# Moving work and stores between engines in a four-layer attention and GLU training kernel

What was changed: the first block of a GLU stage is turned on PE instead of by DMA; stores of turned tiles are issued by SyncE, one later; the transposed load of the down weights is cut in three; small attention weight gradients are made in the tail; copies of attention backward run on ScalarE.

## The chip, the cores and the metric

The kernel runs on one core of one Trainium2 chip. The metric is the device time of one execution in microseconds (us), as the median of several runs. The profile is of one execution. In it PE is TensorE (matmuls), PEld its weight loads, DVE VectorE, ACT ScalarE, POOL GpSimd, SP SyncE. SyncE and POOL also issue DMA transfers. A tile whose name ends in `_ps` lies in PSUM, the memory that this kernel's matmuls write and sum in; "turned" means transposed; the granted clock is the share of full speed at which PE was allowed to run.

## The reference

Four residual layers, forward and backward: linear attention, GLU, linear attention, GLU, with the same weights in both attentions and in both GLUs. The outputs are the result and the gradients of x and of the five weights. Everything is bfloat16. S = 2048, D = 512, F = 1376, 32 heads of 16.

```python
phi = lambda t: jnp.where(t > 0, t + 1, jnp.exp(t)) + 1e-6
pq, pk = phi(q), phi(k)
kv  = jnp.einsum("bhsd,bhse->bhde", pk, v)
z   = jnp.einsum("bhsd->bhd", pk)
num = jnp.einsum("bhqd,bhde->bhqe", pq, kv)
den = jnp.einsum("bhqd,bhd->bhq", pq, z)[..., None] + 1e-6
attention = (num / den)...reshape(B, S, D) @ wo          # cut
glu = (sigmoid(x @ w_gate) * (x @ w_up)) @ w_down

x = A_x
x = x + attention(layernorm(x))      # layer 0
x = x + glu(layernorm(x))            # layer 1
x = x + attention(layernorm(x))      # layer 2
x = x + glu(layernorm(x))            # layer 3
# the kernel also returns the vjp of all this for grad_out
```

## The kernel before

The sequence is cut into 4 blocks of 4 tiles of 128 rows. Most products of the kernel take a normalised block turned (`hT`), and forward stores many tiles in DRAM for backward. Four parts matter here.

Layer norm after the first layer: POOL makes the negated mean and the power, ACT the squares, DVE applies, and a transposing DMA issued by SyncE turns the block. `pooled` ties stores issued by POOL (`k.st` is POOL) to POOL's powers and products.

```python
            neg = k.small.tile([P, 2], F32, name="ln_neg", bufs=8)
            nc.gpsimd.tensor_scalar(neg[:], k.sums[st // 2][:], -1.0 / D, None, ALU.mult)
            # cut: ScalarE squares and sums with bias=neg
            nc.gpsimd.tensor_scalar(rstd, ss[:], 1.0 / D, EPS_LN, ALU.mult, ALU.add)
            pooled(k, nc.gpsimd.tensor_tensor(rstd, rstd, k.neghalf[:], ALU.pow))
            for i in range(2):
                nc.vector.tensor_scalar(self.h[b][:, j - 1 + i, :], k.xs[st - 1 + i][:], neg[:, i:i + 1],
                                        rstd[:, i:i + 1], ALU.add, ALU.mult)
            nc.sync.dma_start_transpose(out=self.hT[b][:, j - 1:j + 1].rearrange("p a c q -> p (a c) q"),
                                        in_=self.h[b][:, j - 1:j + 1, :].rearrange("p a d -> p (a d)"))
```

Attention's query features and the normalised features `qn`, which a DMA turns and which POOL stores when they have landed:

```python
        nc.vector.tensor_scalar(a_t[:], pe[:, 1], 1.0, EPS, ALU.min, ALU.add)
        nc.gpsimd.tensor_scalar(pe[:, 1], pe[:, 1], 1.0, None, ALU.min)
        for i in range(2):
            nc.vector.scalar_tensor_tensor(pe[:, 0, i, :], qs[i][:], 1.0 + EPS, a_t[:, i, :], ALU.add, ALU.max)
        # cut, in share():
        nc.sync.dma_start_transpose(out=self.qn[b][:, 2 * d2:2 * d2 + 2].rearrange("p c a q -> p (c a) q"),
                                    in_=pe[:, 0].rearrange("p c s -> p (c s)"))
        if d2:
            self.turned.append((self.sv["qn"][b], self.qn[b]))
            self.store_turned()          # k.st.dma_start of the oldest waiting tile
```

GLU forward of layer 1 stores its slopes and products as soon as they are made:

```python
            hh, sd = glu(k, ln.hT[b], fc)
            nc.sync.dma_start(out=sv["sd"][b, fc], in_=flat(sd))
            store_hh(k, sv, b, fc, hh)   # k.st.dma_start, so POOL
```

Attention backward has a first pass over the blocks (gradients of the queries), a middle part (small matrices), and a second pass (gradients of the keys, values and the layer's input). The gradients of `wo` and of the value weights, which need only small products, are made at the start of the second pass. Layer 2 comes first and stores its share in `dwp`; layer 0 reads that share back and adds it:

```python
    for c in range(NDC):
        ps = k.ps.tile([P, D], F32, name="dw_ps", tag="bank")
        nc.tensor.matmul(ps[:], lhsT=kv[:, c, :], rhs=C[:, c, :], start=True, stop=True)
        put(k, ps[:], "wo", rows(c), slice(0, D), mode, stg)
    # cut: 4 transposes of dkv, then 16 matmuls and 4 more put for the value weights
def put(k, ps, nm, rs, cs, mode, pool=None):
    # cut
    if mode == "last":
        old = pool.tile([P, D], BF16, name="dw_old", **({} if pool is k.p_dst else dict(bufs=1)))
        nc.sync.dma_start(out=old[0:r, 0:w], in_=k.dwp[nm][rs, cs])
        nc.vector.tensor_tensor(new[0:r, 0:w], ps, old[0:r, 0:w], ALU.add)
    else:
        nc.scalar.copy(new[0:r, 0:w], ps)
    k.st.dma_start(out=dst, in_=new[0:r, 0:w])
```

After both backward attentions comes the tail, which is almost only matmuls of large weight gradients.

Of the kernel before, what the change touches and what calls it, by code (L numbers as in the profile page):

```python
# [16 lines left out]
D = 512  # L17
# [38 lines left out]
def kernel(  # L56
# [41 lines left out]
    for l in range(4):  # L98
        d = dict(h=dram.tile([S, D], BF16, name=f"sv_h{l}"))
        if l % 2 == 0:  # L100
# [6 lines left out]
            d["kv"] = dram.tile([P, NDC * P], BF16, name=f"sv_kv{l}")  # L107
        else:
# [8 lines left out]
    k.dwp = {nm: dram.tile(list(k.w_in[nm].shape), BF16, name=f"dwp_{nm}") for nm in k.w_in}  # L117
    k.rstd = [k.keep.tile([P, NST], F32, name=f"rstd{l}") for l in range(4)]
    k.A = {l: {} for l in (0, 2)}
    k.n_pool, k.waiting = 0, []  # L120
# [35 lines left out]
def build_mask(k):  # L156
    nc = k.nc

    after(k, nc.gpsimd.memset(k.bdmask[:], 1.0), k.last_pool)
# [35 lines left out]
def pooled(k, ins):  # L195

    k.n_pool += 1
    k.last_pool = ins
    while k.waiting and k.waiting[0][0] <= k.n_pool:
        after(k, k.st.dma_start(**k.waiting.pop(0)[1]), ins)  # L200


def store_later(k, lag=4, **kw):
    k.waiting.append((k.n_pool + lag, kw))
# [5 lines left out]
class LN:  # L210
# [12 lines left out]
    def one(self, st):  # L223
# [5 lines left out]
        if l == 0:  # L229
# [9 lines left out]
            if 0 < st < 6:  # L239
                after(k, add, k.last_pool)  # L240
            pooled(k, nc.gpsimd.tensor_tensor(rstd, rstd, k.neghalf[:, 0:1], ALU.pow))
# [9 lines left out]
        elif j % 2:  # L251
# [3 lines left out]
            nc.gpsimd.tensor_scalar(neg[:], k.sums[st // 2][:], -1.0 / D, None, ALU.mult)  # L255
# [6 lines left out]
            pooled(k, nc.gpsimd.tensor_tensor(rstd, rstd, k.neghalf[:], ALU.pow))  # L262
            for i in range(2):
                nc.vector.tensor_scalar(self.h[b][:, j - 1 + i, :], k.xs[st - 1 + i][:], neg[:, i:i + 1],
                                        rstd[:, i:i + 1], ALU.add, ALU.mult)
            nc.sync.dma_start_transpose(out=self.hT[b][:, j - 1:j + 1].rearrange("p a c q -> p (a c) q"),
                                        in_=self.h[b][:, j - 1:j + 1, :].rearrange("p a d -> p (a d)"))
        if j == NB - 1:
            k.st.dma_start(out=by_tile(k.sv[l]["h"], b * NB, NB), in_=self.h[b][:])
            if l % 2 == 0:  # L270
                store_later(k, out=k.sv[l]["hT"][b], in_=flat(self.hT[b]))
# [11 lines left out]
def forward(k):  # L283
    nc, tc = k.nc, k.tc
    with ExitStack() as ctx:
# [28 lines left out]
        for b, fc in b_both(k, 3, lns[3], ctx):  # L314
            if b == 0:
                next(second, None)
                if next(second, None) is None and actx:
                    actx.close()
                    wb = w_pool(k, "wb")
                    k.wuT = wb.tile([P, NFC, D], BF16, name="wuT")  # L320
                    k.wgT = wb.tile([P, NFC, D], BF16, name="wgT")
                    load_b_bwd(k, k.wuT, "wu", k.last_mul)
                    load_b_bwd(k, k.wgT, "wg", k.last_mul)
                    actx = None
        assert not k.waiting
# [18 lines left out]
def load_b_fwd(k, pks):  # L344
    nc, wd = k.nc, k.w_in["wd"]
    after(k, nc.gpsimd.memset(k.wd[0:FDUP, NFC - 1, :], 0.0), k.last_pool)
# [4 lines left out]
         nc.sync.dma_start(out=k.wd[FDUP:P, NFC - 1, :], in_=wd[n:F, :]))  # L351

# [16 lines left out]
class AFwd:  # L369


    def __init__(self, k, l, ln):
        self.k, self.l, self.ln, self.sv = k, l, ln, k.sv[l]
        self.pks, self.turned, self.pe, self.RD, self.qn, self.rd = [], [], {}, {}, {}, {}

    def store_turned(self):

        dst, t = self.turned.pop(0)
        self.k.st.dma_start(out=dst, in_=flat(t))

    def keys(self, st):
# [16 lines left out]
        if j == NB - 1:  # L398
            self.turned.append((self.sv["pkT"][b], self.pkT))
            if b:  # L400
                self.store_turned()
# [33 lines left out]
    def query(self, b, d2):  # L435
# [12 lines left out]
        nc.gpsimd.tensor_scalar(pe[:, 1], pe[:, 1], 1.0, None, ALU.min)  # L448
# [18 lines left out]
    def share(self, b, d2):  # L467
# [14 lines left out]
        if d2:  # L482
            self.turned.append((self.sv["qn"][b], self.qn[b]))
            self.store_turned()

    def slope(self, b, d2):
        k, pe = self.k, self.pe[b, d2]
        k.nc.vector.tensor_tensor(pe[:, 1], pe[:, 1], self.rd[b, d2][:], ALU.mult)
# [29 lines left out]
    def second(self, nxt):  # L518
# [36 lines left out]
        if l == 2:  # L555
            k.wdT = k.p_wa.tile([P, NDC, F], BF16, name="wdT", tag="wkvo")
            nc.sync.dma_start_transpose(out=k.wdT[:], in_=k.w_in["wd"])
# [15 lines left out]
        self.query(2, 1)  # L573
        self.out(1, 2, nxt)
        self.out(1, 3, nxt)
        self.slope(1, 1)
        self.den(2)
        yield True
# [8 lines left out]
        dst, t = self.turned.pop(0)  # L587
        store_later(k, out=dst, in_=flat(t))


def glu(k, hT, fc):
# [13 lines left out]
    pooled(k, nc.gpsimd.tensor_tensor(sd[:, 1, :], sd[:, 1, :], hh[:], ALU.mult))  # L605
# [3 lines left out]
def store_hh(k, sv, b, fc, hh):  # L609
    p0, f1 = (FDUP if fc == NFC - 1 else 0), min((fc + 1) * P, F)  # L610
    k.st.dma_start(out=sv["hhT"][fc * P:f1, b * SB:(b + 1) * SB], in_=hh[p0:P])


def b_fwd(k, l, ln, nxt):
    nc, sv = k.nc, k.sv[l]
    hhs = {}
# [9 lines left out]
    for b in range(NBLK):  # L626
        hhs[b] = []
        for fc in range(NFC):
            hh, sd = glu(k, ln.hT[b], fc)
            hhs[b].append(hh)  # L630
            nc.sync.dma_start(out=sv["sd"][b, fc], in_=flat(sd))
            store_hh(k, sv, b, fc, hh)
            if fc == 1 and b:
                down(b - 1)
            yield b, fc
    down(NBLK - 1)
# [10 lines left out]
def b_both(k, l, ln, ctx):  # L647
# [17 lines left out]
    for b in range(NBLK):  # L665
# [4 lines left out]
        for fc in range(NFC):  # L670
# [9 lines left out]
            store_hh(k, sv, b, fc, hh)  # L680
# [31 lines left out]
def backward(k):  # L712
    nc, tc = k.nc, k.tc
    with ExitStack() as ctx:
# [23 lines left out]
        k.p_set, k.p_dst = pool("dw_set_end", 6), pool("dw_stage_end", 6)  # L738
        for i, a in ((0, 1), (1, 0), (1, 1), (2, 0), (2, 1)):
            joint(i, a)  # L740
# [6 lines left out]
        for i, nm in ((1, "dkT"), (0, "dqT")):  # L747
            dw_cols(k, "wqkv", i * D, (0, D), [(h2, sv[2][nm]), (h0, sv[0][nm])])

# [77 lines left out]
def a_bwd(k, l, final):  # L827
    with ExitStack() as ctx:
        CT, dzp = a_bwd1(k, l, ctx)
        a_bwd2(k, l, final, ctx, CT, dzp)  # L830


def a_bwd1(k, l, ctx):
    nc, sv, A = k.nc, k.sv[l], k.A[l]
    big = ctx.enter_context(k.tc.tile_pool(name=f"ab_big{l}", bufs=1))
# [3 lines left out]
    k.big2 = ctx.enter_context(k.tc.tile_pool(name=f"ab_big2{l}", bufs=1))  # L839
    with k.tc.tile_pool(name=f"ab_ph1{l}", bufs=2) as ph1:  # L840
        CT_ps = [k.ps2.tile([P, D], F32, name="CT_ps", tag="dwbank") for _ in range(NDC)]
        late = []

        def sums(b, g_t, qn):
            for jc in range(NDC):
                for j in range(NB):
                    nc.tensor.matmul(CT_ps[jc][:], lhsT=g_t[:, j, jc * P:(jc + 1) * P], rhs=qn[:, :, j, :],
                                     start=(b == 0 and j == 0), stop=(b == NBLK - 1 and j == NB - 1))

        def soft(b, dc, dq, u_t, qp, rp, dqT):  # L850
            t_ps = k.ps.tile([P, SB], F32, name="t_ps", tag="bank")
            nc.tensor.matmul(t_ps[:], lhsT=k.bdmask[:], rhs=u_t[:], start=True, stop=True)
            w_t = ph1.tile([P, SB], BF16, name="w_t")
            nc.vector.scalar_tensor_tensor(w_t[:], t_ps[:], A["nz"][:, dc:dc + 1], dq[:], ALU.mult, ALU.add)  # L854
            nc.gpsimd.tensor_tensor(dqT[:, dc, :], w_t[:], rp[:, dc, :], ALU.mult)  # L855
            nc.vector.scalar_tensor_tensor(u_t[:], t_ps[:], -1.0, qp[:, dc, :], ALU.mult, ALU.mult,
                                           accum_out=dzp[:, dc, b:b + 1])
            if dc == NDC - 1:
                k.st.dma_start(out=by_chunk(sv["dqT"], b), in_=dqT[:])

        for b in range(NBLK):
            g_t = k.p_h.tile([P, NB, D], BF16, name="ga_t", tag="h_t")
            gT = k.p_hT.tile([P, NB, NDC, P], BF16, name="gaT_t", tag="hT_t")
            for j in range(NB):
                nc.scalar.copy(g_t[:, j, :], k.xs[b * NB + j][:])
                if j % 2 == 0:
                    tp = k.ps.tile([P, 2 * NDC, P], BF16, name="T_ps", tag="bank")
                for c in range(NDC):
                    nc.tensor.transpose(tp[:, j % 2 * NDC + c, :], g_t[:, j, c * P:(c + 1) * P], k.ident[:])
                if j % 2:  # L870
                    nc.scalar.copy(gT[:, j - 1:j + 1].rearrange("p a c q -> p (a c) q"), tp[:])
            qr = k.p_sh.tile([P, 2, NDC, SB], BF16, name="qr_l", tag="sh")
            qp, rp = qr[:, 0], qr[:, 1]
            nc.sync.dma_start(out=flat(qr), in_=sv["qr"][b])
            qn = k.p_h.tile([P, NDC, NB, P], BF16, name="qn_l", tag="h_t")
            nc.sync.dma_start(out=flat(qn), in_=sv["qn"][b])
            if b == 0 and l == 2:
                nc.sync.dma_start_transpose(out=k.woT[:], in_=k.w_in["wo"])
                nc.sync.dma_start_transpose(out=k.wqkvT[:], in_=k.w_in["wqkv"])
            if b == NBLK - 1 and l == 2:  # L880
                nc.sync.dma_start_transpose(out=k.wdT[:], in_=k.w_in["wd"])
            dqT = ph1.tile([P, NDC, SB], BF16, name="dqT_t")
            for dc in range(NDC):
                ps = k.ps.tile([P, SB], F32, name="dq_ps", tag="bank")
                mm4(k, ps[:], lambda c: MT[:, c, dc * P:(dc + 1) * P], lambda c: gT[:, :, c, :])
                dq = ph1.tile([P, SB], BF16, name="dq_sb", bufs=3)
                nc.scalar.copy(dq[:], ps[:])
                u_t = ph1.tile([P, SB], BF16, name="u_t", bufs=3)
                nc.vector.tensor_tensor(u_t[:], dq[:], qp[:, dc, :], ALU.mult)
                late.append((b, dc, dq, u_t, qp, rp, dqT))  # L890
                if len(late) > 2:
                    soft(*late.pop(0))
# [225 lines left out]
```

## Time and profile before

| | before |
|---|---|
| median of the first 3 runs | 1251.42 us (1248.57 to 1255.02) |
| profiled execution, span | 1240.5 us |
| PE busy, and not busy in the span | 1109.0 us, 131 us |
| mean granted PE clock | 0.968 |
| POOL busy | 454.0 us |

The page, its first part (busy us, share of the span) and two rows of its second part (the span in 40 slices, busy tenths, and the granted clock in tenths):

```profile
PE 1109.0 (89%) x5536; PEld 511.5 (41%) x5536; DVE 548.4 (44%) x968; ACT 513.2 (41%) x1020; POOL 454.0 (37%) x563
...
PE   5978899986697999999779799989799999999997
...
PEclk9998899999799999999999899999899899999999
```

PE is the limit almost everywhere; the dips (slices 10 and 11, and some single ones) are where time is to be had. The dips have a second price: after a wait of 6.8 us, which ended at 130.0 us, four matmuls took 1.86 us where four take 1.02 to 1.03 elsewhere, and the granted clock from 130 to 134 us was 0.50. The clock record of this trace holds only full and half, and 81 us of half (the mean of 0.968 alone would give 2 x 0.032 x 1240.5 = 79 us).

PE's waits (waiter, line and releaser: total us, times, longest us):

```profile
PE den_ps L458 <- DVE pe_t L450: 14.6, 5, 11.5
PE g_ps L179 <- DMA hT_t<-h_t: 11.5, 2, 8.3
PE u_ps L179 <- ACT rd_t L475: 7.4, 2, 6.8
...
PE dh_ps L704 <- DMA wgT<-in_B_w_gate_dram: 4.6, 1, 4.6
```

The list names only the last link of a chain. The timeline shows the chain (start us, duration us, engine and line, what, and in brackets the engine's idle time before it and what ended that). From layer 2 into layer 3, before:

```profile
306.23 0.64 POOL L379 DMA_DIRECT2D sv_qn_125<-qn_t  x1 [9.97 <-DMA qn_t<-pe_t]
...
308.72 1.28 DVE L264 TENSOR_SCALAR h_t<-x_90,ln_neg,rstd_140 128x512 bf16<-128x512 f32 x1 [7.68 <-POOL rstd_140 L262]
...
313.95 0.26 PE L458 MATMUL den_ps<-pe_t,Z_t 128*32 128x128 bf16 x1 [11.50 <-DVE pe_t L450]
...
314.66 2.03 SPq L266 DMA_TRANSPOSE hT_t<-h_t  x1
...
322.50 0.61 PE L179 MATMUL g_ps<-hT_t,wg 128*128 128x512 bf16 x1 [8.29 <-DMA hT_t<-h_t]
```

POOL stands for 10 us at a store whose tile is still being turned. The rest of the layer norm, with its power, stands right behind it in POOL's order, so DVE waits 7.7 us for it. DVE makes the feature that PE needs only behind that (from 312.3 us, though ACT had finished its input at 301.1), and PE waits 11.5 us for it. Then the block has to be turned by a DMA, and PE waits another 8.3 us.

The same pattern occurs at the end of layer 1, which I did not see before predicting. (For this store the profile names no releaser, only "issue"; that POOL waited there for the turn of `pkT` is read from the same store in e14 below.) Timeline of before:

```profile
241.99 0.57 POOL L379 DMA_DIRECT2D sv_pkT_123<-pkT  x1 [4.20 <-issue]
242.58 0.24 POOL L255 TENSOR_SCALAR ln_neg<-x_sum 128x2 f32<-128x2 f32 x1
242.86 0.72 ACT L259 ACTIVATE ln_junk<-x_100,ln_neg 128x512 bf16<-128x512 f32 x1 [6.87 <-POOL ln_neg L255]
...
252.12 1.02 PE L179 MATMUL k_ps<-wkvo,hT_t 128*128 128x512 bf16 x4 [3.00 <-DVE pk_t L394]
```

And the small gradients of layer 0, which wait for the read-back:

```profile
893.13 0.69 DVE L1031 TENSOR_TENSOR dw_new<-dw_ps,dw_old 128x512 bf16<-128x512 f32 x1 [7.31 <-DMA dw_old<-dwp_wo]
...
893.88 0.58 PE L990 MATMUL dw_ps<-dkv,ET_t 128*128 128x128 bf16 x4 [5.50 <-DVE dw_new L1031]
...
894.68 4.67 PE L1006 MATMUL dh_ps<-wqkvT,dkT_t 128*128 128x512 bf16 x11
```

I measured stages by PE's own milestones, from the first matmul of one kind to the first of another. The table of stretches has for each: from:to, length, busy us (and instructions) of PE, PEld, DVE, ACT and POOL, then the granted clock, the DMA share and GB/s. Five stages of before, in order: layer 1 from its first down product to layer 2's first query; layer 2 from its first output product to the first gate product of layer 3; layer 3's backward; and the second passes of attention backward of layer 2 and of layer 0 (from the first product with `Nv`; see e10 for what this milestone hides):

```profile
140.80:272.42 131.62, 125.19 (x630) 56.68 (x629) 63.08 (x125) 82.44 (x156) 77.08 (x113) 1.00 0.70 200
...
288.44:322.50 34.06, 12.39 (x58) 4.91 (x56) 18.05 (x36) 9.45 (x22) 14.54 (x19) 0.74 1.02 247
...
387.07:579.01 191.94, 186.50 (x856) 83.98 (x857) 88.06 (x143) 94.53 (x192) 64.83 (x81) 0.99 0.40 114
...
646.39:703.54 57.15, 52.86 (x247) 23.84 (x246) 36.12 (x55) 31.10 (x76) 26.45 (x27) 0.94 0.54 159
...
884.32:944.30 59.98, 52.62 (x246) 23.86 (x245) 36.53 (x60) 24.74 (x59) 28.68 (x29) 0.94 0.60 184
```

### The profile page before, as it was taken

How to read it: one execution, taken by the hardware profiler on the slowest of the kernel's cores; microseconds unless marked ns; L12 is line 12 of the kernel's file. 1: busy time of each engine (PE TensorE's matmuls, PEld its weight loads, DVE VectorE, ACT ScalarE, POOL GpSimd, SP SyncE). 2: the span in 40 equal slices, each digit the busy share in tenths (PEclk: the TensorE clock that was granted, in tenths of full speed). 3: DMA queues.
4: the chain of work that ended last, by engine and by line, in shares of the span. 5: the costliest groups of instructions: out<-in, count | busy, mean ns of one | idle time of the engine just before them, and what ended most of it. 6: DMA issues, size and time to landing. Idle time of an engine off the chain costs nothing. (4 is left out here: it accounts for less than half of the span.)

```text
span 1240.5 us, 15505 instructions
## 1 busy us (share of the span) xinstructions
PE 1109.0 (89%) x5536; PEld 511.5 (41%) x5536; DVE 548.4 (44%) x968; ACT 513.2 (41%) x1020; POOL 454.0 (37%) x563
## 2 busy tenths in 40 slices
PE   5978899986697999999779799989799999999997
PEld 2433344443233444444334344444344344654443
DVE  6577444556562545453568645548575000000000
ACT  4456677635471738273524634355245000100100
POOL 6367677625662435250434412125255000100000
PEclk9998899999799999999999899999899899999999
DMA  6997776668679334244694785678953997899772
GB/s 222 243 229 213 205 232 194 197 164 190 176 220 227 115 107 140 66 141 118 208 324 144 177 257 185 210 262 276 266 183 96 276 230 154 165 266 209 172 179 53
DMA packets 372461, 238.54 MB, mean 192 GB/s; under 512 B 286368, under 2 KB 339840, under 8 KB 371360
## 3 DMA queue, kind: packets, MB, share of 16 engines
q1 hardware_dynamic: 352432, 172.50, 55.3%
q0 software_dynamic: 19952, 65.06, 15.0%
q8 instruction: 43, 0.70, 0.2%
q14 instruction: 34, 0.28, 0.1%
HBM read 68.45 MB, written 99.12 MB: 135 GB/s over the span
## 5 line engine op out<-in xcount | busy, mean ns | idle before, releaser
L1070 PE MATMUL dw_ps<-set_t,h_all 128*128 128x512 bf16 (+1 forms) x1024 | 207.3, 366 | 3.1 <-DMA set_t<-sv_ddT_116 3.1
L1070 PEld LDWEIGHTS <-h_all 128*128 128x128 bf16 x1024 | 100.9, 99 | 109.3 <-issue 7.2
L605 POOL TENSOR_TENSOR sd_t<-sd_t,hh_t 128x512 bf16<-128x512 bf16 x88 | 105.6, 1200 | 105.5 <-ACT sd_t L604 45.0
L1033 ACT CAST dw_new<-dw_ps 128x512 bf16<-128x512 f32 (+2 forms) x51 | 25.3, 578 | 259.6 <-issue 184.0
L1034 POOL DMA_DIRECT2D out_dram<-dw_new x51 | 27.4, 543 | 262.6 <-ACT dw_new L1033 225.5
L179 PE MATMUL g_ps<-hT_t,wg 128*128 128x512 bf16 x352 | 93.6, 389 | 12.3 <-DMA hT_t<-h_t 11.5
L179 PE MATMUL u_ps<-hT_t,wu 128*128 128x512 bf16 x352 | 92.8, 387 | 7.7 <-ACT rd_t L475 7.4
L179 PE MATMUL dhh_ps<-gT_t,wdT 128*128 128x512 bf16 x352 | 89.8, 379 | 0.0
L179 PE MATMUL y_ps<-wd,hh_t 128*128 128x512 bf16 x352 | 78.0, 379 | 2.0 <-DVE hh_t L603 2.0
L1084 PE MATMUL dw_ps<-g_all,set_t 128*128 128x512 bf16 (+1 forms) x352 | 76.3, 379 | 1.7 <-DMA set_t<-sv_hhT_115 1.7
L794 PE MATMUL dh_ps<-wuT,dd_t 128*128 128x512 bf16 x176 | 66.8, 379 | 7.0 <-DVE dd_t L815 4.3
L603 DVE SCALAR_TENSOR_TENSOR hh_t<-sd_t,u_ps 128x512 bf16<-128x512 bf16 x88 | 60.1, 683 | 25.3 <-ACT sd_t L602 23.4
L794 PE MATMUL dh_ps<-wgT,dd_t 128*128 128x512 bf16 x176 | 66.7, 379 | 0.0
L602 ACT ACTIVATE sd_t<-th_t,onef 128x512 bf16<-128x512 f32 x88 | 63.4, 721 | 3.2
L179 PEld LDWEIGHTS <-wg 128*128 128x128 bf16 x352 | 34.8, 100 | 67.4 <-DMA hT_t<-h_t 20.2
L604 ACT ACTIVATE sd_t<-th_t,onef 128x512 bf16<-128x512 f32 x88 | 62.3, 708 | 0.0
L855 POOL TENSOR_TENSOR dqT_t<-w_t,qr_l 128x512 bf16<-128x512 bf16 x32 | 38.0, 1198 | 63.9 <-DVE w_t L854 63.4
L601 ACT ACTIVATE th_t<-g_ps 128x512 f32<-128x512 f32 x88 | 51.3, 587 | 15.6 <-PE g_ps L179 14.8
L179 PEld LDWEIGHTS <-wu 128*128 128x128 bf16 x352 | 35.0, 100 | 52.5 <-issue 13.7
L676 DVE TENSOR_TENSOR sd_t<-dhh_t,sd_t 128x1024 bf16<-128x1024 bf16 x44 | 33.4, 761 | 51.1 <-POOL sd_t L605 51.1
L815 DVE TENSOR_TENSOR dd_t<-dhh_t,sh_t 128x1024 bf16<-128x1024 bf16 x44 | 32.1, 737 | 53.2 <-ACT dhh_t L813 47.9
L704 PEld LDWEIGHTS <-sd_t 128*128 128x128 bf16 x352 | 34.6, 99 | 49.2 <-issue 8.7
(539 smaller groups left out, 1926.6 us busy)
## 6 DMA issues: line engine op xcount, KB each, us to landing
sv_sd_118<-sd_t SPq DMA_DIRECT2D x44, 256.0 KB, 2.3
sv_ddT_131<-sd_t SPq DMA_DIRECT2D x40, 256.0 KB, 2.2
sv_ddT_116<-dd_t SPq DMA_DIRECT2D x40, 256.0 KB, 4.0
sh_t<-sv_sd_118 SPq DMA_DIRECT2D x8, 1024.0 KB, 7.0
out_dram<-dw_new POOLq DMA_DIRECT2D x42, 128.0 KB, 4.0
sv_hhT_115<-hh_t POOLq DMA_DIRECT2D x40, 128.0 KB, 3.0
sv_hhT_130<-hh_t POOLq DMA_DIRECT2D x40, 128.0 KB, 2.1
sv_qr_109<-pe_t POOLq DMA_DIRECT2D x8, 512.0 KB, 5.6
```

What stands on the lines that cost most here:

```text
L179: i = k.nc.tensor.matmul(out, lhsT=lhs(c), rhs=rhs(c), start=(c == 0), stop=(c == n - 1))
L601: nc.scalar.activation(th[:], g_ps[:], ACT.Tanh, scale=-0.5)
L602: nc.scalar.activation(sd[:, 0, :], th[:], ACT.Identity, bias=k.onef[:], scale=-1.0)
L603: nc.vector.scalar_tensor_tensor(hh[:], sd[:, 0, :], 0.5, u_ps[:], ALU.mult, ALU.mult)
L604: nc.scalar.activation(sd[:, 1, :], th[:], ACT.Identity, bias=k.onef[:])
L605: pooled(k, nc.gpsimd.tensor_tensor(sd[:, 1, :], sd[:, 1, :], hh[:], ALU.mult))
L676: k.last_mul = nc.vector.tensor_tensor(dd[:], dhh[:].unsqueeze(1).to_broadcast([P, 2, SB]), dd[:], ALU.mult)
L704: k.nc.tensor.matmul(dh_ps[:], lhsT=dds[fc][:, a, rows(j)], rhs=(k.wuT, k.wgT)[a][:, fc, :], start=(i == 0), stop=(i == 2 * NFC - 1))
L794: nc.tensor.matmul(acc[b][j][:], lhsT=dd[:, a, rows(j)], rhs=(k.wuT, k.wgT)[a][:, fc, :], start=(fc == 0 and a == 0), stop=(fc == NFC - 1 ...
L855: nc.gpsimd.tensor_tensor(dqT[:, dc, :], w_t[:], rp[:, dc, :], ALU.mult)
L1070: k.nc.tensor.matmul(ps[ic][:, 0:w], lhsT=h_t[:, ic * P:(ic + 1) * P], rhs=t, start=(i == 0 and st == 0), stop=(i == len(srcs) - 1 and st ...
L1084: k.nc.tensor.matmul(p[0:r, :], lhsT=t[:, f:f + r], rhs=g_t, start=(i == 0 and st == 0), stop=(i == len(srcs) - 1 and st == NST - 1))
```

## The change

The intent is to take PE's waits away: keep POOL clear of stores that wait, turn the block that PE needs at once on PE itself, cut the transposed load of the down weights in three, and take the small weight gradients with their read-back out of attention backward. The diff, cut to its core:

```diff
-def pooled(k, ins):                       # and store_later: stores by POOL, tied to its powers (cut)
+def store_turned(k, dst, t):
+    flush_turned(k)
+    k.turned.append((dst, t))
+
+def flush_turned(k):
+    while k.turned:
+        dst, t = k.turned.pop()
+        k.nc.sync.dma_start(out=dst, in_=flat(t))
@@ layer norm
-            nc.gpsimd.tensor_scalar(neg[:], k.sums[st // 2][:], -1.0 / D, None, ALU.mult)
+            nc.scalar.mul(neg[:], k.sums[st // 2][:], -1.0 / D)
-            pooled(k, nc.gpsimd.tensor_tensor(rstd, rstd, k.neghalf[:], ALU.pow))
+            nc.gpsimd.tensor_tensor(rstd, rstd, k.neghalf[:], ALU.pow)
-            nc.sync.dma_start_transpose(out=self.hT[b]...)
+            if b or l == 2:
+                nc.sync.dma_start_transpose(out=self.hT[b]...)
+    def turn(self, j):                    # first block of a GLU: 8 transposes on PE, one copy
+        tp = k.ps.tile([P, 2 * NDC, P], BF16, name="T_ps", tag="bank")
+        for i in range(2):
+            for c in range(NDC):
+                nc.tensor.transpose(tp[:, i * NDC + c, :], self.h[0][:, j + i, c * P:(c + 1) * P], k.ident[:])
+        nc.scalar.copy(self.hT[0][:, j:j + 2].rearrange("p a c q -> p (a c) q"), tp[:])
@@ attention forward
-        nc.gpsimd.tensor_scalar(pe[:, 1], pe[:, 1], 1.0, None, ALU.min)
-        k.nc.vector.tensor_tensor(pe[:, 1], pe[:, 1], self.rd[b, d2][:], ALU.mult)
+        k.nc.vector.scalar_tensor_tensor(pe[:, 1], pe[:, 1], 1.0, self.rd[b, d2][:], ALU.min, ALU.mult)
-            nc.sync.dma_start_transpose(out=k.wdT[:], in_=k.w_in["wd"])
+            turn_wd(k, k.wdT, 0)          # a third; the others after den(2) and in layer 3
+        nxt.turn(0)                       # and nxt.turn(2) two outputs later
@@ GLU forward of layer 1
-            nc.sync.dma_start(out=sv["sd"][b, fc], in_=flat(sd))
-            store_hh(k, sv, b, fc, hh)
+            if late:
+                store()                   # both stores of the chunk before, on SyncE
+            late.append((b, fc, hh, sd))
@@ attention backward
-            (nc.vector.tensor_copy if jc % 2 else nc.scalar.copy)(CT[:, jc, :], CT_ps[jc][:])
+        nc.scalar.copy(CT[:, jc, :], CT_ps[jc][:])          # Nv likewise
+            if dc == 1 and b + 1 < NBLK:
+                grads(b + 1)              # copies and turns of the next block's gradients
-    for c in range(NDC): ... put(k, ps[:], "wo", ..., mode, stg)       # small gradients (cut)
@@ tail
+def dw_small(k):                          # both layers summed in PSUM, inputs turned by DMA
+            nc.tensor.matmul(wo[c][:], lhsT=kv[:, c, :], rhs=C[:, c, :], start=(i == 0), stop=(i == 1))
```

Not shown: the forward stores that were held back by a count of POOL's operations (`store_later`) are no longer held back, and attention backward loads its tiles in another order and from other buffer pools.

## The prediction

> **What bounds the kernel.** TensorE. The page gives PE 1109 us busy of a 1240.5 us span (89%), the other engines at most 44%. Time can come only from PE's 131 us of idle, and from the half-speed clock after it [...]. The trace agrees: after a 6.8 us wait at 130 us four matmuls take 1.9 us instead of 1.03. The list of waits and the timeline put PE's idle in four places:
>
> - Attention of layer 2 into the second GLU (296 to 330 us): 11.5 us (den_ps for pe_t), 8.3 us (g_ps for the transposing DMA of hT_t), 20 us at half clock. The chain: POOL waits 10.0 us in order at the store of qn_t for its transposing DMA; rstd behind it comes late, DVE waits 7.7 us for rstd, PE for DVE; then the transposing DMA of hT (4.7 us).
> - The same place of layer 0 (84 to 136 us): 2.7, 3.2 and 6.8 us. POOL is late here too, and beside its minimum (2.8 us, 16 times) a 0.55 us DVE instruction takes 1.8 us.
> - Attention backward, twice (578 to 692; 825 to 915): 18 and 13 us, among them 5.5 and 1.9 us for dw_old loads and 3.1 us for Wp.
> - The start of the weight-gradient tail: 3.1 us for set_t.
>
> **What the change does.**
> - First block of each GLU turned on PE: 32 more transposes, 69 ns each (8.8 us for 128), and 4 ScalarE copies of 1.0 us, in place of DMA landings.
> - Stores of hT, pkT, qn, hhT (layer 1) and sd on SyncE, one later: POOL no longer waits for a transpose, loses 26 us of issuing for hhT; SyncE no longer waits 60 us for fresh sd.
> - POOL's minimum goes into the DVE slope: 45 us leave POOL, DVE pays perhaps 0.4 us for each of 16 (estimated from 0.69 us now).
> - wo and wv gradients move into the tail, both layers summed in PSUM: 40 transposes and the dwp round trip go; about 5 us of matmuls move. PE's work hardly changes.
> - Backward gradients of block b+1 are turned within block b; CT and Nv copies all on ScalarE, 0.6 us each.
>
> **Sum** (estimates from those waits and half the half-clock time that goes with them): layer 2 forward -19; layer 0 forward -11; attention backward -7 and -10; tail start -4; new waits (transposed loads and bank reuse in the tail, serial CT copies, mask building between the first rstd, SyncE order) +8. Total -43 us.
>
> **Predicted: 1208 us**, 8 in 10 between 1188 and 1232. Faster by over 2%: 0.84; within: 0.13; slower: 0.03.
>
> **What would show it.** PE idle near 95 us, busy 1095 to 1112, mean clock above 0.975 (0.968 now). POOL busy falls from 454 to about 350 us. The waits den_ps for pe_t and g_ps for hT_t fall from 26 us to under 8. No dw_old wait. DVE slope about 1.1 us. The GLU stages and the tail hardly change in length.
>
> **What would make it wrong.** The chain behind hT (sums, squares, rstd, h_t, turn, copy) may itself be late, with more on ScalarE, so that the wait only changes its name. SyncE, in order, may block transposes or loads behind a store that waits. Loads of wdT, wuT or wgT may be the next wait in layer 3 (wgT 4.6 us now). In attention backward the loads of qr and qn, or DVE, may be the true limit, so that removing other waits gives little.

The sum is -19 - 11 - 7 - 10 - 4 + 8 = -43 us. The +8 for new waits is worked out from no measured number.

## The result, and the profile after

| | before | after |
|---|---|---|
| median (4 runs each, beside each other) | 1249.99 us (1247.62 to 1255.02) | 1170.14 us (1169.37 to 1171.55) |
| ratio, 95% interval | | 0.9357 (0.9325 to 0.939) |
| span of the profiled execution | 1240.5 us | 1167.3 us |
| PE busy, not busy | 1109.0, 131 us | 1085.6, 82 us |
| mean granted clock | 0.968 | 0.987 |
| POOL busy | 454.0 us | 368.0 us |

Ratios here and below are the mean time of one kernel's runs over that of the other's of the same rounds, so they are not quite the ratios of the medians quoted. Outputs are correct. The gain is 80 us in the times and 73 us in the profiled executions, because before's profiled execution is one of its quickest. A later control run of the same new kernel gave 1174.29 us, so a difference of 4 us between batches of runs means nothing.

The page of after, the same rows (some matmul records are missing: 5439 matmuls against 5528 weight loads, so PE's idle time is a little overstated):

```profile
PE 1085.6 (93%) x5439; PEld 508.4 (44%) x5528; DVE 535.8 (46%) x952; ACT 518.1 (44%) x1046; POOL 368.0 (32%) x451
...
PE   4978999998899999997998899989999999989997
...
PEclk8999999999899999999999999989999999999999
```

The dip in slices 10 and 11 is gone. The clock record holds 34 us at half rate, 47 less than before. PE's waits in after (the longest of all, cut here, are 11.5 us in the set-up for `h_t`, 8.2 us in attention backward for `u_t` and 7.1 us for `pe_t` in `y_ps`; before had 10.2, 5.8 and 5.1 us there):

```profile
...
PE den_ps L470 <- DVE pe_t L462: 4.0, 6, 1.2
...
PE g_ps L180 <- ACT hT_t L283: 3.3, 2, 2.4
```

The den_ps and g_ps waits are 7.3 us together where they were 26.1, and no wait for a read-back is left. The timeline of after where layer 2 enters layer 3:

```profile
277.25 0.69 POOL L263 TENSOR_TENSOR rstd<-rstd,neghalf 128x2 f32<-128x2 f32 x1
...
280.07 0.61 PE L282 MATMUL T_ps<-ident,h_t 128*128 128x128 bf16 x8
...
280.72 1.01 ACT L283 COPY hT_t<-T_ps 128x1024 bf16<-128x1024 bf16 x1 [0.30 <-PE T_ps L282]
...
281.78 0.59 PE L180 MATMUL g_ps<-hT_t,wg 128*128 128x512 bf16 x2 [0.89 <-ACT hT_t L283]
```

From the last power to the first gate product 4.5 us pass (277.25 to 281.78); in before it was 14.7 us (307.85 to 322.50). At the end of layer 1 the same store and the same mean as in the timeline of before with `pkT` now stand on engines where neither holds the other up; timeline of after:

```profile
220.91 0.20 ACT L256 ACTIVATE ln_neg<-x_sum 128x2 f32<-128x2 f32 x1 [3.22 <-DVE x L386]
...
222.57 0.33 SPq L205 DMA_DIRECT2D sv_pkT<-pkT  x1
```

The five stretches of after that answer to those of before:

```profile
125.94:250.51 124.57, 123.35 (x621) 56.53 (x629) 67.43 (x131) 85.09 (x169) 54.73 (x63) 1.00 0.80 222
...
266.37:281.78 15.41, 12.74 (x68) 6.02 (x71) 14.81 (x30) 11.97 (x27) 5.24 (x10) 1.00 1.02 257
...
347.75:534.41 186.66, 184.11 (x840) 83.72 (x856) 87.53 (x144) 94.86 (x192) 64.07 (x79) 1.00 0.44 119
...
593.22:643.81 50.59, 46.29 (x205) 20.59 (x208) 33.13 (x51) 25.82 (x64) 22.10 (x18) 0.97 0.52 146
...
827.97:872.65 44.68, 44.52 (x205) 20.25 (x208) 31.30 (x48) 24.58 (x59) 24.61 (x20) 1.00 0.39 140
```

All stages of the two profiled executions, beside the terms of the prediction (layer 0's attention backward is counted from its first product with `MT`, layer 2's from its first transpose):

| stage | before us | after us | measured | predicted |
|---|---|---|---|---|
| start to the first down product of layer 1 | 140.8 | 125.9 | -14.9 | -11 |
| rest of layer 1 (GLU forward) | 131.6 | 124.6 | -7.0 | 0 |
| layer 2, query start to first output product | 16.0 | 15.9 | -0.2 | 0 |
| layer 2, first output product to layer 3's first gate product | 34.1 | 15.4 | -18.7 | -19 |
| layer 3 forward part | 64.6 | 66.0 | +1.4 | part of +8 |
| layer 3 backward | 191.9 | 186.7 | -5.3 | 0 |
| attention backward of layer 2 | 124.5 | 109.4 | -15.1 | -7 |
| layer 1 backward | 129.9 | 131.4 | +1.5 | 0 |
| attention backward of layer 0 | 110.9 | 97.5 | -13.4 | -10 |
| tail | 296.2 | 294.7 | -1.5 | -4, and part of +8 |
| sum | | | -73.2 | -43 |

### The profile page after: what moved, and what is told of

Same layout as the page of the kernel before. It is cut to its first block, busy times and chain, and to the rows that moved or that the text cites. A ratio compares the mean times of both kernels' runs of the same rounds, so it can differ in the third digit from the quotient of the medians.

```text
span 1167.3 us, 15363 instructions
## 1 busy us (share of the span) xinstructions
PE 1085.6 (93%) x5439; PEld 508.4 (44%) x5528; DVE 535.8 (46%) x952; ACT 518.1 (44%) x1046; POOL 368.0 (32%) x451
## 3 DMA queue, kind: packets, MB, share of 16 engines
q1 hardware_dynamic: 362032, 189.93, 63.7%
## 5 line engine op out<-in xcount | busy, mean ns | idle before, releaser
L1094 PE MATMUL dw_ps<-set_t,h_all 128*128 128x512 bf16 (+1 forms) x1007 | 203.9, 362 | 2.2 <-ACT dw_new L1029 1.3
L618 POOL TENSOR_TENSOR sd_t<-sd_t,hh_t 128x512 bf16<-128x512 bf16 x88 | 106.6, 1217 | 123.1 <-ACT sd_t L617 52.5
L792 POOL TENSOR_TENSOR x<-t_sb,x 128x512 f32<-128x512 f32 x48 | 71.3, 1496 | 148.9 <-ACT c1n L784 120.5
L782 ACT ACTIVATE t_sb<-dh_ps,rstd 128x512 f32<-128x512 f32 x64 | 43.5, 681 | 124.0 <-PE dh_ps L725 94.9
L616 DVE SCALAR_TENSOR_TENSOR hh_t<-sd_t,u_ps 128x512 bf16<-128x512 bf16 x88 | 59.9, 681 | 24.9 <-ACT sd_t L615 22.7
L818 PE MATMUL dh_ps<-wuT,dd_t 128*128 128x512 bf16 x167 | 64.4, 385 | 7.2 <-DVE dd_t L839 3.7
L818 PEld LDWEIGHTS <-dd_t 128*128 128x128 bf16 x352 | 34.5, 99 | 50.9 <-DVE dd_t L839 9.1
L892 POOL TENSOR_TENSOR dqT_t<-w_t,qr_l 128x512 bf16<-128x512 bf16 x32 | 37.7, 1188 | 56.4 <-DVE w_t L891 56.0
```

The costliest lines, as they stand in the source:

```text
L616: nc.vector.scalar_tensor_tensor(hh[:], sd[:, 0, :], 0.5, u_ps[:], ALU.mult, ALU.mult)
L618: nc.gpsimd.tensor_tensor(sd[:, 1, :], sd[:, 1, :], hh[:], ALU.mult)
L782: nc.scalar.activation(t_sb[:], dh_ps, ACT.Identity, scale=rstd, accum_out=c1[:])
L792: nc.gpsimd.tensor_tensor(k.xs[st][:], t_sb[:], up, ALU.add)
L818: nc.tensor.matmul(acc[b][j][:], lhsT=dd[:, a, rows(j)], rhs=(k.wuT, k.wgT)[a][:, fc, :], start=(fc == 0 and a == 0), stop=(fc == NFC - 1 ...
L892: nc.gpsimd.tensor_tensor(dqT[:, dc, :], w_t[:], rp[:, dc, :], ALU.mult)
```

## The experiments

Fifteen kernels were run in four batches, each for 3 rounds beside the kernel before; all were correct. The batches ran on three chips (e1 to e4 and e13 to e15 on one, e5 to e8 and e9 to e12 on two others), so a time is best compared by its ratio to before, which ran beside it. Before was 1248.51 to 1250.59 us in these batches. Each run has one trace, so a stage is one measurement. "+" is against the new kernel's 1170.1 us; with the control's 1174.3 in mind, I read nothing into less than 5 us of time, and use the stages for smaller things. The theories' letters are those of the expectations.

| run | what | median us | ratio (95%) |
|---|---|---|---|
| e3_fwd_only | only the forward half changed | 1201.53 | 0.9589 (0.954, 0.9638) |
| e4_bwd_only | only the backward half changed | 1223.97 | 0.9778 (0.9733, 0.9823) |
| e1_no_turn | no turn on PE | 1184.64 | 0.9477 (0.9426, 0.9529) |
| e2_turned_pool | turned stores on POOL | 1184.08 | 0.9466 (0.9423, 0.9509) |
| e7_neither | e1 and e2 | 1194.65 | 0.9561 (0.9521, 0.9601) |
| e8_wd_whole | down weights loaded in one piece | 1183.54 | 0.9479 (0.9434, 0.9524) |
| e5_min_pool | minimum on POOL | 1170.81 | 0.9369 (0.9331, 0.9406) |
| e6_hh_pool | layer 1's stores as before | 1175.24 | 0.9411 (0.9363, 0.946) |
| e9_not_ahead | gradients not one block ahead | 1172.86 | 0.9393 (0.9342, 0.9444) |
| e10_small_back | small gradients not in the tail | 1192.51 | 0.9545 (0.9499, 0.959) |
| e11_neg_pool | mean on POOL | 1178.97 | 0.9435 (0.939, 0.9481) |
| e12_copies_split | copies shared with VectorE | 1172.61 | 0.9405 (0.9353, 0.9457) |
| e13_neg_and_turned | e2 and e11 | 1195.79 | 0.9567 (0.9533, 0.9601) |
| e14_neg_turned_hh | e2, e6 and e11 | 1204.23 | 0.9631 (0.959, 0.9672) |
| e15_new_again | control, the new kernel | 1174.29 | 0.9398 (0.9364, 0.9431) |

### Halves: e3_fwd_only and e4_bwd_only

Each takes the code of one half from the new kernel and the other half from before.

```diff
 # e3: set-up and forward of the new kernel
-def backward(k): ...      # new
+def backward(k): ...      # as before, with dwp
```

> The changed forward pass with the backward pass and tail of the kernel before. If the parts add up as the two traces split them (45 of 73 us in the trace before the first transpose of attention backward, scaled to 80 us of time): 1196 to 1206 us. If the backward part was sped up by what the forward leaves (DMA queues, late stores): below 1190 us.

```diff
 # e4: set-up and forward of before
-def backward(k): ...      # as before
+def backward(k): ...      # new
```

> The forward pass of the kernel before with the changed backward pass and tail. If the parts add up: 1214 to 1224 us, and with the forward-only run the two savings sum to 80 us within 6. If they lean on each other, the sum of the two savings misses 80 us by over 10.

Measured: the forward half alone saved 49 us (1250.59 to 1201.53), the backward half alone 26.6 us. The sum is 75.7 of 80, so by the times the halves hardly act on each other. In e3 the stages up to attention backward were those of the new kernel within 1.5 us. In e4 the second pass of layer 0 was that of the new kernel (44.7 us, 61.0 in e3), but attention backward of layer 2 was 118.5 us, between before's 124.5 and the new kernel's 109.4, and 125.3 in e3: there only 6 of the 15 us came with the backward half alone. Why the rest needs both halves is not shown; e4's profiled execution was also its slowest.

Layer 3's backward was 186.6 us in e3 and 190.9 in e4, so its 5 us belong to the forward half. The traces show what it waited for. Timeline of before:

```profile
375.02 0.59 POOL L200 DMA_DIRECT2D sv_qn_125<-qn_t  x1
...
394.60 3.82 PE L704 MATMUL dh_ps<-wgT,sd_t 128*128 128x512 bf16 x11 [4.57 <-DMA wgT<-in_B_w_gate_dram]
```

And of after:

```profile
320.42 0.34 SPq L205 DMA_DIRECT2D sv_qn<-qn_t  x1
...
334.32 5.71 SPq L376 DMA_TRANSPOSE wgT<-in_B_w_gate_dram  x1
```

The turned up and gate weights go into the space of the attention's buffers, so their loads must wait for the last store of `qn`. In before that store was one of those held back (`store_later`): POOL issued it 52.5 us after layer 3's first gate product, the profile names it as what released SyncE's first load (at 55.6 us), and the gate weights landed at 72.1 us, for which PE waited. In the new kernel the store goes out at 38.6 us and the gate weights land at 61.2. e4 has before's times (52.7 and 71.3), e14, where POOL issues the store but does not hold it back, the new kernel's (38.8 and 60.8). So the held-back store is the likely cause of the 5 us; no run undoes it alone.

### The turn on PE: e1_no_turn

```diff
-            if b or l == 2:
+            if True:
                 nc.sync.dma_start_transpose(out=self.hT[b]...)
-        nxt.turn(0)
-        nxt.turn(2)
```

> The changed kernel (about 1170 us), but the first block of each GLU is turned by the transposing DMA again, as in the kernel before. Theory A (POOL's in-order wait at the store of qn is what made the 19 us at the entry of the second GLU; the turn on PE is worth only the landing of the DMA): 1174 to 1186 us, the wait of den_ps for pe_t stays under 3 us, and a wait of g_ps for the DMA of hT_t of 3 to 8 us returns at each of the two entries. Theory B (the DMA turn itself was the delay): 1190 us or more, with the second GLU starting at least 10 us later.

Measured: +14.5 us, and the stage from layer 2's first output product to layer 3's first gate product went from 15.4 to 29.4 us. Timeline of e1_no_turn:

```profile
277.51 1.00 DVE L265 TENSOR_SCALAR h_t<-x,ln_neg,rstd 128x512 bf16<-128x512 f32 x2 [0.22 <-POOL rstd L263]
...
289.14 1.46 SPq L268 DMA_TRANSPOSE hT_t<-h_t  x1
...
295.34 1.89 PE L180 MATMUL g_ps<-hT_t,wg 128*128 128x512 bf16 x4 [15.80 <-DMA hT_t<-h_t]
```

The block is ready at 278.5 us, but SyncE issues its transpose only at 289.1: transposes of qn, a piece of the down weights and a store stand before it in SyncE's order. So the turn on PE saves more than a DMA's landing; it takes the block out of a queue. The turn is worth nothing at the first GLU: from layer 0's first output product to layer 1's first down product 54.7 us with it (56.5 in the control) and 54.7 without. So neither theory held as written: the time is in Theory A's range, but PE's wait at the second GLU is 15.8 us and not 3 to 8, the stage is 14 us longer as Theory B said, and at the first GLU only 0.9 us of wait returned.

### The stores: e2_turned_pool, and both: e7_neither

```diff
-        k.nc.sync.dma_start(out=dst, in_=flat(t))
+        k.st.dma_start(out=dst, in_=flat(t))       # POOL
```

> The changed kernel, but the stores of hT, pkT and qn go out from POOL again (still one later); all else as changed. Theory A: POOL waits again in order for a transposing DMA, rstd is late, and 12 to 25 us return, so 1182 to 1195 us, with a POOL wait of 5 us or more at the store of qn. Theory B: under 6 us return, because the first block no longer needs the DMA turn: 1168 to 1176 us.

Measured: +13.9 us. The first attention lost 9 us (22.0 + 32.7 to 28.8 + 34.9) and the stage into layer 3 9.5 us (15.4 to 24.9). Timeline of e2_turned_pool:

```profile
294.02 0.62 POOL L205 DMA_DIRECT2D sv_qn<-qn_t  x1 [7.31 <-DMA qn_t<-pe_t]
...
295.74 1.00 DVE L265 TENSOR_SCALAR h_t<-x,ln_neg,rstd 128x512 bf16<-128x512 f32 x2 [5.24 <-POOL rstd L263]
```

It is before's chain again: the store holds the power, the power holds DVE. For 7.3 us POOL had a power to make and stood at a store (the power's input was ready 10 us before the store went out), and DVE stood 5.2 us for the power.

> The changed kernel with both taken back: the first blocks turned by DMA and the stores of hT, pkT and qn on POOL. Each alone returned 14 us. Theory C (two queues that each hold up the same chain, so that a part of the gain is shared): the entry of the second GLU (first attention output of layer 2 to the first gate product) is back to 32 to 36 us against 15.4 changed and 34.1 before, and the whole takes 1189 to 1197 us. If the two are independent: the entry takes 38 us or more and the whole 1198 us or more.

Measured: +24.5 us, where the two singles add to 28.4. In the stage into layer 3 the two overlap (29.4 and 24.9 us alone, 31.4 together, just under Theory C's 32 to 36). The time is in Theory C's range.

### The split load: e8_wd_whole

```diff
-            turn_wd(k, k.wdT, 0)
+            nc.sync.dma_start_transpose(out=k.wdT[:], in_=k.w_in["wd"])
-        if l == 2:
-            turn_wd(k, k.wdT, 1)
-                if fc == 2:
-                    turn_wd(k, k.wdT, 2)
```

> The changed kernel, but the transposed load of wd for layer 3 is one transfer again at the place of the first of the three. Theory: SyncE, in order, then holds the transposes of qn behind an 8.8 us transfer, but with the first block turned on PE nothing in the chain to the GLU needs SyncE, so under 4 us return (1168 to 1174 us). If the split itself is what counts: 6 us or more (1176 us or more).

My expectation fell: +13.4 us. In the traces the stage into layer 3 took 22.7 us instead of 15.4, and the first pass of layer 2's attention backward 47.5 instead of 43.7. The second I leave aside, since other runs scatter there as much (44.4 in the control, 47.3 in e12). Timeline of e8_wd_whole for the first:

```profile
267.63 8.13 SPq L566 DMA_TRANSPOSE wdT<-in_B_w_down_dram  x1
...
286.03 1.08 ACT L455 ACTIVATE pe_t<-q_ps 128x512 bf16<-128x512 f32 x2 [9.12 <-DMA sv_MT<-MT_t]
...
289.07 1.01 PE L180 MATMUL g_ps<-hT_t,wg 128*128 128x512 bf16 x2 [8.16 <-ACT hT_t L283]
```

And the DMA list of e8_wd_whole for 262 to 300 us (tile, engine, transfers, KB each if known, median us from issue to landing):

```profile
sv_MT<-MT_t POOLq DMA_DIRECT2D x1, 512.0 KB, 16.9
...
wdT<-in_B_w_down_dram SPq DMA_TRANSPOSE x1, 23.9
```

The feature tile `pe_t` reuses the buffer of `MT_t`, whose store of 512 KB took 16.9 us to land beside the whole load. In the new kernel the same store, issued at the same 269.1 us, took 6.1 us, and a third of the load 7.5; in before, beside the same whole load, the store took 10.8 us. ACT stood at the feature for 9.1 us, the copy of the turned block came behind it (at 287.0 us, though PE had turned the first half by 278.5), and PE waited 8.2 us for that copy. From 272 to 278 us the DMA moved 174 GB/s in e8 and 322 in the new kernel. So with the whole load beside it the store took 16.9 us and not 6.1, and the turn on PE did not help here, where its copy waited.

### What turned out not to matter: e5_min_pool, e6_hh_pool, e9_not_ahead, e12_copies_split

```diff
 # e5
+        nc.gpsimd.tensor_scalar(pe[:, 1], pe[:, 1], 1.0, None, ALU.min)
-        k.nc.vector.scalar_tensor_tensor(pe[:, 1], pe[:, 1], 1.0, self.rd[b, d2][:], ALU.min, ALU.mult)
+        k.nc.vector.tensor_tensor(pe[:, 1], pe[:, 1], self.rd[b, d2][:], ALU.mult)
```

> The changed kernel, but the minimum of the slope is taken on POOL again (2.8 us each, 16 times), the slope on DVE is the plain product. Theory D (the minimum makes POOL late and stretches DVE beside it): 4 to 12 us return, 1174 to 1182 us, most of it between the first GLU matmul and the first down product of layer 1 and in the entries of the GLUs. Rival: once POOL no longer waits for transposes it has slack enough, and the change is worth under 3 us either way (1167 to 1173 us).

Measured: 1170.81 us, no effect on the time. Theory D's loss at the entry of the second GLU did come (18.1 us against 15.4), but layer 3's forward part was shorter by as much or more (60.0 against 64.6 in the control and 66.0); why is not shown. Before, DVE's apply beside POOL's minimum took up to 1.84 us instead of 0.55, and I had taken that for a cost. Moving the minimum to DVE did not help the time, though POOL is 42.7 us less busy in the new kernel than in e5; why is not shown.

```diff
 # e6
-            if late:
-                store()
-            late.append((b, fc, hh, sd))
+            nc.sync.dma_start(out=sv["sd"][b, fc], in_=flat(sd))
+            store_hh(k, sv, b, fc, hh, k.st)
```

> The changed kernel, but in layer 1 hhT goes out from POOL and sd from SyncE at once, as in the kernel before. The two traces differ by 7.0 us between the first down product of layer 1 and the first query product of layer 2, which the prediction did not count. If these stores are its cause (SyncE blocked behind fresh sd tiles, POOL late with 0.6 us issues): 5 to 9 us return there, 1175 to 1180 us. If they are not: under 2 us, 1168 to 1172 us, and that stretch stays at 124.6 us.

Measured: 1175.24 us, in the range of the first theory, but its interval overlaps the control's, and layer 1's stage was 126.0 us against 124.6, far from the 5 to 9 us more that the theory asked for.

```diff
 # e9
-    grads(0)
     for b in range(NBLK):
+        grads(b)
-            if dc == 1 and b + 1 < NBLK:
-                grads(b + 1)
```

> The new kernel, with each block's gradient copies and turns in attention backward again made at the start of their own block instead of one block ahead. Theory F (turning ahead is what shortened the first pass of attention backward of layer 2, 48.9 to 43.7 us): that stage goes back to 47 to 49 us, the same pass of layer 0 (39.0 in the new kernel, 36.6 before) stays within 2 us, and the time is 1173 to 1178. Rival (the stage gained from loads that land earlier and from a higher granted clock, not from the order of the turns): the stage stays at 43 to 45 us and the time is within 3 us of 1170.

Measured: 1172.86 us, not apart from the control. The first pass of layer 2 rose to 46.7 us (43.7 and 44.4 in the two runs of the new kernel), that of layer 0 fell to 36.2 (39.0 and 37.6). The other kernels with the turns ahead have 43.6 to 47.9 us and 34.2 to 38.5, so neither change is clear of the scatter.

```diff
 # e12
-        nc.scalar.copy(CT[:, jc, :], CT_ps[jc][:])
+        (nc.vector.tensor_copy if jc % 2 else nc.scalar.copy)(CT[:, jc, :], CT_ps[jc][:])
-        nc.scalar.copy(Nv[:, c, :], ps[:])
+        (nc.vector.tensor_copy if c % 2 else nc.scalar.copy)(Nv[:, c, :], ps[:])
```

> The new kernel, with the copies of C and Nv out of PSUM in attention backward shared between VectorE and ScalarE again instead of all on ScalarE. My expectation: no effect, 1167 to 1173, and the stages between the first pass and the first product with Nv (15.1 us in layer 2, 13.8 in layer 0) within 1.5 us. Rival (the copies on ScalarE are part of the gain): the two stages grow by 2 to 4 us each and the time is 1174 to 1180.

Measured: 1172.61 us, and the two middle parts were 16.8 and 15.2 us against 15.5 and 14.8 in the control (the first is 1.7 above the new kernel's 15.1, just outside my range). No effect that I can tell.

### The small gradients: e10_small_back

```diff
 # in the second pass, from before: loads of kv and E, 16 + 4 transposes, 4 + 16 matmuls, 8 results a layer
+    old = ...; nc.sync.dma_start(out=old[0:r, 0:w], in_=k.dwp[nm][rs, cs])     # layer 0 adds layer 2's share
-                dw_small(k)
```

> The new kernel, with the small attention weight gradients made inside attention backward again, as before (transposes of C and dkv on PE, 36 matmuls a layer, results of layer 2 stored, read back and added in layer 0), and none in the tail. Theory G (the move took 22 us out of the two second passes of attention backward, 6.5 and 15.3, and gave back about 5 in the tail; in layer 0 half of the 15 was a wait for the read-back and its buffers): the second pass of layer 0 goes from 44.7 to 56 to 61 us, that of layer 2 from 50.6 to 55 to 58, the tail after the gradient rows from 146 to about 141, and the time is 1182 to 1190. Rival (the passes became shorter because of the copies on ScalarE and the order of the loads): the time is within 5 us of 1170 and the pass of layer 0 stays under 50.

Measured: 1192.51 us, +22.4; a little more than Theory G's range, as is layer 2's pass. The second pass went from 44.7 to 61.0 us in layer 0 and from 50.6 to 59.1 in layer 2. The start of the tail took 4.1 us more, its end 4.9 us less. Timeline of e10_small_back:

```profile
846.00 0.69 DVE L1059 TENSOR_TENSOR dw_new<-dw_ps,dw_old 128x512 bf16<-128x512 f32 x1 [7.54 <-DMA dw_old<-dwp_wo]
...
846.74 0.59 PE L1019 MATMUL dw_ps<-dkv,ET_t 128*128 128x128 bf16 x4 [5.72 <-DVE dw_new L1059]
```

This is the largest single part of the backward half. The milestone hides something: in before and in e10, 16 products of the next block's keys (`dpk_ps`, 3.6 to 4.1 us) come after the first product with `Nv`, in the new kernel before it. So I take the middle part and the second pass together, from the first product `dkvT_ps`, and split the length into PE's idle and busy time:

| from `dkvT_ps` to the end of the second pass | before | e10 | new |
|---|---|---|---|
| layer 0: length (idle, busy) | 74.3 (10.0, 64.3) | 73.7 (9.9, 63.7) | 58.5 (0.4, 58.1) |
| layer 2: length (idle, busy) | 75.6 (9.8, 65.9) | 73.4 (8.5, 64.9) | 65.7 (5.7, 60.0) |

So taking the small gradients back costs layer 0 15.2 us, of which 9.5 are idle time (5.7 and 3.1 us of it waits for `dw_new`, the result that needs the read-back) and 5.7 PE work. It costs layer 2, which reads nothing back, 7.7 us, of which 2.8 are idle time and 4.9 PE work. The small products with their transposes are 3.2 and 3.4 us of this work. The rest is that the same large products took longer, as the 11 after the wait: 0.35 us each in e10 (3.88 us) and 0.42 in before (4.67 us), against 0.23. In the tail, summed in PSUM and turned by DMA, the same gradients are 3.8 us of matmuls for both layers.

### Layer 1's 7 us: e11_neg_pool, e13_neg_and_turned, e14_neg_turned_hh, and the control

```diff
 # e11
-            nc.scalar.mul(neg[:], k.sums[st // 2][:], -1.0 / D)
+            nc.gpsimd.tensor_scalar(neg[:], k.sums[st // 2][:], -1.0 / D, None, ALU.mult)
```

> The new kernel, with the negated mean of the forward layer norms on POOL again instead of ScalarE. Theory H (POOL was late in the kernel before because it stood at stores of turned tiles; with those gone its place doesn't matter): layer 1's GLU stage from the first down product to layer 2's first query stays at 124.6 us within 1.5, and the time is within 4 us of 1170. Rival (having the mean on ScalarE, which no store holds up, is what took the 7 us out of that stage, 131.6 to 124.6): the stage goes to 129 to 132 us and the time to 1175 to 1182.

Measured: the stage stayed at 125.6 us, as Theory H expected. The time, 1178.97 us, is in the rival's range, though its interval overlaps the control's. In the trace the loss is in the first attention, 25.0 + 35.6 us against 22.0 + 32.7 (22.4 + 34.1 in the control).

So for layer 1's stage no single part counted: stores on POOL left it at 124.8, the stores of layer 1 at 126.0, the mean on POOL at 125.6. Three more kernels asked whether they count together.

```diff
 # e13: e2 and e11 together; e14: e2, e6 and e11 together; e15: nothing changed
```

> The new kernel with two things undone at once: stores of turned tiles issued by POOL, and the negated mean of the forward layer norms on POOL. Each alone left layer 1's GLU stage (first down product to layer 2's first query, 131.6 us before, 124.6 in the new kernel) at 124.8 and 125.6. Theory I (the two act together: only where the mean is computed by the engine that stands at the stores does a late store hold up ScalarE and VectorE): the stage goes to 128 to 132 us with a PE wait of 2 to 4 us for the feature tile of the keys, and the time is over 1188. Rival (they don't act together): the stage stays under 126.5 us and the time is the sum of the two singles, 1181 to 1188... the singles cost about 14 and 5 to 9.

> The same two things undone, and the stores of the activation product of layer 1 on POOL too, with the slopes stored from SyncE at once, so that POOL has all stores and the mean, as in the kernel before. Theory I with the extra store issues on POOL: the stage is 130 to 133 us, all of the 7 us, and the time is 1190 to 1205. Rival (the 7 us lie in something else of the forward change, such as the minimum on POOL or the order forced between stores and powers): the stage stays under 128 us.

> A control: the new kernel unchanged, beside the two others on the same chip. All theories expect 1167 to 1173 us and a ratio of 0.933 to 0.939; a larger number would mean that differences of 2 to 5 us between my batches are differences between runs, not between kernels.

Measured: in e13 the stage went to 133.1 us, in e14 to 136.6, and in the control it was 124.3. Both are somewhat above Theory I's ranges and above before's 131.6, so these kernels lose something more that before did not; what, is not shown. The times were 1195.79, 1204.23 and 1174.29 us. (The rival's time range in e13's expectation was added up wrongly: 1170 plus 14 plus 5 to 9 is 1189 to 1193. The time therefore hardly tells the two apart; the stage does.) Timeline of e14_neg_turned_hh:

```profile
243.84 0.56 POOL L205 DMA_DIRECT2D sv_pkT<-pkT  x1 [4.34 <-DMA pkT<-pk_t]
...
244.70 0.72 ACT L260 ACTIVATE ln_junk<-x,ln_neg 128x512 bf16<-128x512 f32 x1 [6.85 <-POOL ln_neg L256]
...
253.96 1.02 PE L180 MATMUL k_ps<-wkvo,hT_t 128*128 128x512 bf16 x4 [3.00 <-DVE pk_t L409]
```

These are before's lines almost to the digit: ACT stood 6.87 us for the mean there and 6.85 here, PE 3.00 us in both (2.54 us in e13). In e2 POOL also stood at this store (13.7 us in three waits), but ACT had the mean already and went on. In e11 POOL had the mean but did not stand at stores. The 7 us needed both, each of these kernels in one trace.

## Why the prediction was wrong

It said 1208 us (1188 to 1232) and -43; the result was 1170 us and -80. The direction and the chains it named were right. Its largest term, layer 2 into layer 3, was -19 and measured -18.7, and e1, e2, e7 and e8 show that chain part by part. What failed:

- **"The GLU stages and the tail hardly change in length."** The tail did hardly change as a whole (296.2 to 294.7 us), the GLU stages did: layer 1's forward lost 7.0 us and layer 3's backward 5.3. The 7.0 are shown by e13 and e14: I had read the late mean and power on POOL as a matter of the two places with large waits, and had not looked at the end of layer 1, where POOL stood at a store of `pkT` and ACT behind it. PE's losses there were many and small (3.0, 2.0 and some under 1 us). For the 5.3 us, PE waited 4.6 us for the turned gate weights and 1.7 for the up weights in before, and not in after. I had listed the 4.6 us as a wait that might remain, and not seen that the change takes it away: the loads stood behind a held-back store (see Halves). All kernels with the new forward have 185.8 to 186.7 us there, e4 has 190.9; no run undoes this store alone.
- **"Attention backward -7 and -10."** Measured -15.1 and -13.4. I had counted the waits and half of the half-rate time that goes with them, and held that "PE's work hardly changes". That is what failed, and the term that was mis-sized is the small gradients. From the first product `dkvT_ps` to the end of the second pass layer 0 lost 15.8 us, 9.6 of PE's idle time and 6.2 of its work; layer 2 lost 9.9, 4.1 idle and 5.9 work. e10 gives back 15.2 and 7.7 of these. Of the work, 3.6 and 3.5 us are the small products and their transposes, which took PE time in these passes and came back smaller (3.8 us for both layers together); the rest is large products that ran slower. The other 5.2 us of layer 2 lie in its first pass and are open: kernels with the same code have 43.6 to 47.9 us there, and layer 0's first pass was 2.4 us longer than before.
- **The first attention, -11**, measured -14.9. e2 and e11 lost 9 and 6 us there (7 and 4 against the control), so a late POOL is at least part of it. There are also the waits of 3.2 and 6.8 us after which PE ran slower (the first four matmuls took 1.86 us in both cases, not 1.03): in before the clock was 0.87 in the stretch from the first gate product to the first down product (46.0 us), and 1.00 in after (32.7 us).
- **The base.** I worked from before's profile at 1240.5 us. Its runs scatter from 1243 to 1259 us, the new kernel's only from 1169 to 1176. Its slower runs have a lower granted clock (1242.87 us at 0.969, 1256.71 at 0.959), so probably the waits vary from run to run and with them the half rate; only one execution of before was profiled, so this is not shown. The 80 us of the times against the 73 of the profiles are 7 of the 37 us.
- **"New waits ... +8"** was about right in size: layer 3's forward part +1.4 and layer 1's backward +1.5 in length, and 4.6 us at the end of the tail, most of it the moved gradients.
- **What would show it**: the waits under 8 us (7.3), no wait for `dw_old`, POOL near 350 us (368), a clock above 0.975 (0.987) came as written; the slope was a little dearer than 1.1 us (1.21 at least). PE's idle time of 95 us became 82, and its busy time, expected at 1095 to 1112, became 1085.6.

Of the parts, four carry the gain: the turn on PE at the second GLU (14 us when taken out), the stores off POOL (14, and 26 with the mean back on POOL too), the split load (13), and the small gradients (22). Each is against 1170.1 us and 4 us less against the control. They overlap, so they are not to be added. The minimum, the order of the gradient turns and the copies on ScalarE carry nothing that I could measure, and nothing that I undid made the kernel clearly quicker.

## What to carry to other kernels

In these kernels a store was a wait for its tile, and what stood behind it on the engine waited too: POOL stood 9.97 us at one in before and 7.31 us in e2, and DVE then 7.7 and 5.2 us for the power behind it; in e1 about 11 us passed on SyncE from the ready block to the issue of its transpose. So look not at how long the issue takes but at what stands behind it, and don't put a store of a tile that a DMA is still making ahead of the small instructions of a layer norm. When two such delays feed each other, undoing either alone may show nothing (layer 1's stage here), so try them together before calling a part idle. And count the PE time of small products as well as their waits: here the waits and other idle time were 9.6 and 4.1 us in the two layers, and PE's own work 6.2 and 5.9 more, of which 3.8 came back in the tail. Compare what a merged instruction takes, too: on 128x1024 bf16 tiles in SBUF scalar_tensor_tensor took 1.22 us on DVE in after (median of 16), where tensor_tensor took 0.68 and tensor_scalar 0.42. Before comparing stages, check that the same work lies between the milestones in both kernels.
